# A cross-covariance attention and highway kernel: gates of two slots over two PSUM banks, v transposed as 32-bit words, a first chain that reads S from PSUM

## The chip, the cores and the metric

The kernel runs on one core of a Trainium2 chip, in one launch. The metric is the device time of that launch in microseconds. A median of several runs is given, and one further execution was recorded by the hardware profiler; all lines of the profile are of that one.

## The reference

```python
def _attn_ref(q, k, v, tau):              # q, k, v: (4, 6336, 256) float32
    qn = q / (norm(q, axis=1) + 1e-06)    # every channel is normed over the 6336 rows
    kn = k / (norm(k, axis=1) + 1e-06)
    s = kn.transpose(0, 2, 1) @ qn / tau  # (4, 256, 256): channel against channel
    a = softmax(s, axis=-1)
    return v @ a                          # (4, 6336, 256)

def _moe_ref(x, w_h, w_t, b_t):           # x: (25344, 256)
    H = np.maximum(x @ w_h, 0.0)
    T = 1.0 / (1.0 + np.exp(-(x @ w_t + b_t)))
    return T * H + (1.0 - T) * x
```

For each of four batches a 256x256 matrix of sums over all rows of q and k must be complete before the first row of that batch's output can be made. The output is then linear in v up to the gate: x = v a, h = v (a w_h), z = v (a w_t) + b_t, and out = sigmoid(z) relu(h) + (1 - sigmoid(z)) x.

## The kernel before

A batch has 6336 rows: 49 tiles of 128 rows and a rest of 64. Each partition holds 49 consecutive rows, so that a load of several tiles is one run of memory per partition. q, k and v are loaded as groups of tiles (QG, VG) through POOL's DMA queue, which turns f32 into f16 on the way; there are rings of four buffers for q, four for k and three for v. The output goes out through SP's queue, four slots (eight tiles) at a time.

The work on one batch has three parts.

- **Scores** (`emit_score`, L230, L234, L239): for each tile, S += k'q (two matmuls of 256 columns), and the diagonal blocks of the gram matrices of k and q in G (two matmuls of 128 columns each), whose diagonals are the squared norms. For some runs of four tiles (RUNS) the squares are made elsewhere: ACT squares (L448), POOL adds halves (L454), DVE reduces (L461), and PE adds the result up over the partitions at the end (L511). The last TAIL tiles of a batch do all q grams first, then all k grams, then all S.
- **The chain** (`make_chain`): norms from G (DVE, L502), their root (ACT in batch 0, POOL later), inverses (DVE), the inverse norms of q spread over the partitions by an f32 matmul (cq, L548), S copied to SBUF (ACT, L519), logits (DVE, L557), exponentials (ACT, L574), softmax rows into `mr` (DVE, L588), their transposes (PE, L599) and the products with w_h and w_t (PE, L618), copied to `mr` beside the softmax (L629). ACT changes its function table for the exponential and back (L490).
- **Slots**: a slot is a pair of tiles, 25 to a batch and 100 in all. For each, PE transposes v (`emit_transpose`, L293: four f16 matmuls against an identity into one PSUM bank, vtps), DVE or ACT copies that to SBUF (`emit_copy`, L307; ACT where the number of the slot is in ACT_COPY), PE makes z, h and x (`mains`, L317: four matmuls of 256 columns each), ACT makes the gate tt = sigmoid(z) (L358) and seeds the z bank with b_t again (L361), DVE makes o = relu(h) tt (L366) and ux = (tt - 1) x (L376), and POOL subtracts (L399) two slots at a time.

PSUM has eight banks of 2 KiB per partition: S, G, two z banks used in turn, one for vtps, and three (hx0, hx1, hx2) for h and x. S and G of batch 0 join those for h and x after the first chain; the scores of later batches take hx1 and hx2.

The order on each engine is written by a planner inside the kernel: it steps through time with a length for every task, keeps a list of tasks per kind and engine (`queues`), and at each step lets an engine take the first task of the first list that is ready (`step_pe`, `step_act`, `step_dve`, `step_pool`, `step_sp`). What it emits is then the fixed order of that engine. Chain tasks come first. PE then prefers scores up to the due slot (S_END), transposes some slots ahead (LOOKS), then z, h and x. POOL prefers loads to subtractions, and issues them in the list `order` (QOFF and VOFF set how early; the last lines before the sort set the first loads of batch 1, v and the weights). A load into a used buffer waits for the last reader of that buffer. Scores of batch 1 are interleaved with slots 0 to 21, and so on; from about slot 65 on there are slots alone.

Of the kernel before, what the change touches and what calls it, by code (L numbers as in the profile page):

```python
# [15 lines left out]
P = 128  # L16
# [44 lines left out]
def kernel(  # L61
# [33 lines left out]
    QG = [spans(4, 8, 8, 8, 8, 8, 3, 2), spans(4, 4, 12, 12, 12, 5)]  # L95
    QG += [spans(4, 8, 12, 12, 8, 5)] * (B - 2)
    VG = [spans(4, 8, 12, 12, 13)] + [spans(12, 12, 12, 13)] * (B - 1)
    GT = {"q": 12, "k": 12, "v": 13}
    CH = 4
    SQR = {"q": 4, "k": 2}  # L100
    RUNS = {1: {'q': [4, 8, 20, 32, 36, 44], 'k': [0, 8, 24, 28, 32, 40]}, 2: {'q': [0, 8, 12, 16, 20, 24, 28, 36, 40], 'k': [0, 12, 16, 32, 40]}, 3: {'q': [8, 12, 20, 28, 32, 40, 44], 'k': [0, 8, 16, 28, 32, 36]}}
    TAIL = [6, 12, 10, 7]
    SPARE = 0
    QOFF, VOFF = [1.5, 3.0, 4.0, 0.5], [7.5, 3.5, 0.5, 9.5]
    SAHEAD = [0, 0.5, 10.0, 10.5]
    LOOKS = [3, 3, 2, 2]
    HOLD = [2, 1, 1, 5]
    DVE_SUBS = 2
    SINGLES = 8
    ACT_COPY = {3, 14, 21, 22, 26, 34, 36, 39, 40, 44, 45, 51, 53, 54, 58, 61, 63, 64, 72, 77, 81, 83, 84, 88, 91, 96, 98, 99}  # L110
    NEAR = 2
    OUTST = 7
    QRING, VRING, ORING = 4, 3, 7
    TTR, UXR, VTR = 4, 3, 5
# [4 lines left out]
    S_END = [21.5, 42.5, 65.0]  # L119
# [35 lines left out]
    EXP_LAG = 0.6  # L155
# [57 lines left out]
    S_t, G_t = {}, {}  # L213
# [5 lines left out]
    def emit_score(b, j, parts, first, last):  # L219
        if first:  # L220
            tags = ("S", "G") if b == 0 else ("hx1", "hx2")
            S_t[b] = psum_pool.tile([P, 2, C], f32, tag=tags[0], name=f"S{b}")
            G_t[b] = psum_pool.tile([P, 4, P], f32, tag=tags[1], name=f"G{b}")
        nr = REM if j == NS else P
        kk, qq = tile_of("k", b, j), tile_of("q", b, j)
        S, G = S_t[b], G_t[b]
        for c in range(2):
            kc = kk[0:nr, bass.ts(c, P)]
# [4 lines left out]
            if "k" in parts:  # L233
                nc.tensor.matmul(  # L234
                    G[:, c, :], kc, kc, start=begins(b), stop=False, skip_group_check=True,
                )
        for c in range(2 if "q" in parts else 0):
            qc = qq[0:nr, bass.ts(c, P)]
            nc.tensor.matmul(  # L239
                G[:, 2 + c, :], qc, qc, start=begins(b), stop=False, skip_group_check=True  # L240
# [4 lines left out]
    def begins(b):  # L245
        if b in begun:
            return False
        begun.add(b)
# [4 lines left out]
    def make_scores(b):  # L253
# [3 lines left out]
        for parts in "qks":  # L257
# [26 lines left out]
    vT_ps, vT_t = {}, {}  # L284
    slot_of = {pair_of(t): t for t in range(NSLOT)}

    def emit_transpose(t):
        b, i = pair_of(t)
        ps = psum_pool.tile([P, 2, 2, P], f16, tag="vT", name=f"vtps{t}")
        for u, r in enumerate(nrows(i)):  # L290
            vt = tile_of("v", b, 2 * i + u)
            for c in range(2):
# [3 lines left out]
        vT_ps[t] = ps  # L296

    def emit_copy(t, e):
        i = pair_of(t)[1]
# [881 lines left out]
```

## Time and profile before

| what | value |
|---|---|
| median of 3 runs | 271.5 us (270.67 to 274.68) |
| the profiled execution | 270.55 us, of it span 268.8 us |
| PE busy | 246.3 us (92%), 2564 matmuls |
| DVE, ACT, POOL busy | 207.6, 192.9, 206.5 us |
| DMA | 66.08 MB as landed, share about 1 until some 228 us |
| granted TensorE clock | 0.996 |
| z, h and x matmuls (256 columns) | 1200, 273 ns each as recorded |
| transposes of v | 400, 219 ns each as recorded |

The span runs from the first to the last instruction that the profiler saw; the execution's own time is 1.75 us longer. A matmul's recorded length holds its latency, and matmuls overlap, so that the distance from one to the next is shorter than the record. In the lines that follow a group has its line of the kernel, engine, operation, output and inputs, shapes and count, then busy us and mean ns of one, then the idle time of its engine just before it with what ended it. A line of a table by stage has the stage's bounds, its length and for each engine busy us and count; then the granted clock, the share of the DMA engines and GB/s.

### The profile page before, as it was taken

To read this page: it belongs to the slowest core of one execution; us is meant where nothing else is said; L and a number is where in the kernel's file an instruction comes from. 1 tells how busy PE (TensorE), PEld (TensorE's weight loads), DVE (VectorE), ACT (ScalarE), POOL (GpSimd) and SP (SyncE) were. 2 spreads that over 40 slices of the span, in tenths; PEclk is the share of its full clock that TensorE was granted. 3 is DMA by queue.
4 is the path that set the end of the run, shared out by engine and by line. 5 is a ranking of instruction groups with operands and counts; after the bars stand their busy time and mean duration, and the time that the engine had idled before them with its cause. 6 is when DMAs were issued, how large, how long until landed. Compare 5 with 4: busy or idle time off the path is not lost.

```text
span 268.8 us, 6452 instructions
## 1 busy us (share of the span) xinstructions
PE 246.3 (92%) x2564; PEld 213.7 (79%) x2564; DVE 207.6 (77%) x414; ACT 192.9 (72%) x320; POOL 206.5 (77%) x183
## 2 busy tenths in 40 slices
PE   0996886999999999989999999999999999999990
PEld 0696784798889997879989987898988687999780
DVE  2000035869999999889989899889998998999894
ACT  3310025969689978879996798898868987888780
POOL 6133455399989999898899998899966485977880
PEclk9999999999999999999999999999999999999998
DMA  7999999999999999999999999999999999698435
GB/s 215 213 214 212 205 186 212 214 209 220 213 210 213 235 266 220 209 274 213 288 290 307 278 213 226 214 297 302 272 291 356 266 408 399 142 235 355 200 129 215
DMA packets 16143, 66.08 MB, mean 246 GB/s; under 512 B 1777, under 2 KB 4338, under 8 KB 13170
## 3 DMA queue, kind: packets, MB, share of 16 engines
q0 software_dynamic: 11040, 38.67, 73.0%
q1 hardware_dynamic: 4786, 26.22, 24.3%
q10 hardware_dynamic: 288, 0.79, 0.8%
q8 instruction: 20, 0.33, 0.4%
q14 instruction: 9, 0.07, 0.1%
HBM read 78.38 MB, written 25.95 MB: 388 GB/s over the span
## 4 chain that ended last, share of the span: by engine, by line
PE 47%; DMA 29%; POOL 9%; DVE 7%; ACT 3%; issue 3%; DVEq 0%; POOLq 0%; ACTq 0%
DMA k<-in_k_dram 24%; PE x L317 10%; PE h L317 9%; PE zbank L317 9%; PE S L230 7%; PE vtps L293 5%; POOL o L399 4%; DMA out_dram<-o 3%; PE G L234 3%; PE G L239 3%; DVE o L366 2%; DMA qk<-in_k_dram 2%; DVE ux L376 2%; ACT tt L358 1%; POOL q L177 1%
## 5 line engine op out<-in xcount | busy, mean ns | idle before, releaser
L399 POOL TENSOR_TENSOR o<-o,ux 128x1024 f32<-128x1024 f32 (+2 forms) x50 | 111.5, 2233 | 23.4 <-DVE ux L376 20.3
L317 PEld LDWEIGHTS <-vts 128*128 128x128 f16 x1200 | 111.7, 98 | 16.2 <-issue 4.1
L230 PE MATMUL S<-q,k 128*128 128x256 f16 x392 | 73.5, 278 | 12.5 <-ACT k L834 6.3
L358 ACT ACTIVATE tt<-zbank 128x512 f32<-128x512 f32 x100 | 59.4, 596 | 22.0 <-PE zbank L317 15.7
L366 DVE SCALAR_TENSOR_TENSOR o<-h,tt 128x512 f32<-128x512 f32 x96 | 65.6, 684 | 6.0 <-ACT tt L358 3.3
L376 DVE SCALAR_TENSOR_TENSOR ux<-tt,x 128x512 f32<-128x512 f32 (+1 forms) x104 | 68.0, 657 | 2.1 <-PE x L317 2.0
L317 PE MATMUL x<-mr,vts 128*128 128x256 f16 (+1 forms) x400 | 60.5, 273 | 0.3 <-DVE o L366 0.3
L317 PE MATMUL zbank<-mr,vts 128*128 128x256 f16 (+1 forms) x400 | 60.6, 273 | 0.0
L317 PE MATMUL h<-mr,vts 128*128 128x256 f16 (+1 forms) x400 | 60.5, 273 | 0.0
L361 ACT COPY zbank<-btb 128x512 f32<-128x512 f32 x98 | 57.6, 591 | 2.7
L230 PEld LDWEIGHTS <-k 128*128 128x128 f16 x392 | 37.5, 100 | 18.9 <-DMA k<-in_k_dram 7.8
L234 PE MATMUL G<-k 128*128 128x128 f16 x256 | 44.0, 224 | 0.7 <-DVE junk L502 0.7
L293 PE MATMUL vtps<-ident,v 128*128 128x128 f16 x392 | 38.3, 219 | 1.5 <-DVE vts L307 0.7
L307 DVE COPY vts<-vtps 128x512 f16<-128x512 f16 x68 | 28.6, 420 | 7.2 <-PE vtps L293 6.7
L293 PEld LDWEIGHTS <-v 128*128 128x128 f16 x392 | 28.7, 98 | 4.9 <-issue 1.7
L177 POOL DMA_DIRECT2D q<-in_q_dram x25 | 14.2, 570 | 23.0 <-PE G L239 18.6
L502 DVE SCALAR_TENSOR_TENSOR junk<-G,ident 128x128 f32<-128x128 f32 x16 | 4.7, 291 | 31.1 <-PE G L234 30.4
L239 PE MATMUL G<-q 128*128 128x128 f16 x216 | 28.6, 224 | 0.0
L454 POOL TENSOR_TENSOR sqq<-sqq 128x512 f32<-128x512 f32 (+1 forms) x22 | 26.5, 1207 | 0.1
L234 PEld LDWEIGHTS <-k 128*128 128x128 f16 x256 | 24.0, 101 | 1.8 <-issue 1.1
L448 ACT ACTIVATE sqq<-q 128x1024 f32<-128x1024 f16 x22 | 23.0, 1055 | 0.1
L461 DVE TENSOR_REDUCE sqq<-sqq 128x256 f32<-128x768 f32 x22 | 22.6, 1026 | 0.0
(78 smaller groups left out, 214.3 us busy)
## 6 DMA issues: line engine op xcount, KB each, us to landing
out_dram<-o SPq DMA_DIRECT2D x23, 1024.0 KB, 9.8
v<-in_v_dram POOLq DMA_DIRECT2D x11, 768.0 KB, 17.2
q<-in_q_dram POOLq DMA_DIRECT2D x7, 768.0 KB, 15.2
k<-in_k_dram POOLq DMA_DIRECT2D x7, 768.0 KB, 19.3
q<-in_q_dram POOLq DMA_DIRECT2D x9, 512.0 KB, 13.4
k<-in_k_dram POOLq DMA_DIRECT2D x9, 512.0 KB, 15.4
v<-in_v_dram POOLq DMA_DIRECT2D x4, 832.0 KB, 19.1
q<-in_q_dram POOLq DMA_DIRECT2D x4, 256.0 KB, 13.2
```

What stands on the lines that cost most here:

```text
L230: nc.tensor.matmul(S[:, c, :], kc, qq[0:nr, :], start=first and c == 0, stop=last and c == 1)
L234: nc.tensor.matmul(G[:, c, :], kc, kc, start=begins(b), stop=False, skip_group_check=True,)
L239: nc.tensor.matmul(G[:, 2 + c, :], qc, qc, start=begins(b), stop=False, skip_group_check=True)
L293: nc.tensor.transpose(ps[:, u, c, 0:r], vt[0:r, bass.ts(c, P)], ident[0:r, 0:r])
L307: cp(out=sb, in_=ps)
L317: nc.tensor.matmul(dst[0:r, u, :], vT_t[t][:, u, kt, 0:r], mr[:, kt, off : off + C], start=(not seeded and kt == 0 and (u == 0 or i == NPA ...
L358: nc.scalar.activation(out=tts[t], in_=zbank[t % 2], func=Act.Sigmoid)
L361: nc.scalar.copy(out=zbank[t % 2], in_=btb)
L366: nc.vector.scalar_tensor_tensor(out=ot[pr, o0 + us.start : o0 + us.stop, :], in0=hx["h", t][pr, us, :], scalar=0.0, in1=tts[t][pr, us, :] ...
L376: nc.vector.scalar_tensor_tensor(out=uxs[n][pr, 2 * half + us.start : 2 * half + us.stop, :], in0=tts[t][pr, us, :], scalar=1.0, in1=hx["x ...
L399: ins = sub.tensor_tensor(out=dst, in0=dst, in1=uxs[n][pr, us, :], op=AluOp.subtract)
L454: nc.gpsimd.tensor_tensor(out=sq[:, 1 : 1 + half, :], in0=sq[:, 1 : 1 + half, :], in1=sq[:, 1 + CH - half : 1 + CH, :], op=AluOp.add,)
```

## The change

- **Words.** In batches 0 to 2 v is transposed as f32 words, each of which holds two neighbouring f16 channels: two matmuls of 128 columns per slot instead of four. The channels of k are read with a step of two in these batches, so that the rows of `mr` match (`channels`). The transposes of two slots share one bank and are copied by one instruction, in batch 3 too (f16 there).
- **Batch 3 by DMA.** 22 tiles (11 slots) of batch 3's v are transposed from SBUF to SBUF by six DMAs on SP's queue (DT, `emit_dt`), into buffers of the q and k rings.
- **Gates and seeds.** z has one tile over two banks. A gate, and a seed, covers two slots in one instruction of 128x1024, except for the pairs in ZSPLIT (27 of 50 for the gate).
- **Chain.** The copy of S is gone; the logits read S in PSUM, and cq is copied instead (cqs, on the engine in SPREAD). The q grams of batch 0 have a bank of their own (hx0). The engines of the other copies are set by CENG.
- **Squares.** Other runs (32 instead of 39), and the number of tiles that POOL adds is set per batch (POOLED): 17 additions instead of 39.
- **Lists and numbers.** Groups of loads are cut anew (85 loads of q, k and v by POOL instead of 67), the first loads have another order (FIRSTS), PE's list of z is kept apart from that of h and x, and most of the planner's numbers are new.

```diff
-    QG = [spans(4, 8, 8, 8, 8, 8, 3, 2), spans(4, 4, 12, 12, 12, 5)]
-    QG += [spans(4, 8, 12, 12, 8, 5)] * (B - 2)
-    VG = [spans(4, 8, 12, 12, 13)] + [spans(12, 12, 12, 13)] * (B - 1)
+    QSZ = [[4, 6, 1, 9, 3, 1, 11, 1, 4, 9], [5, 4, 6, 5, 10, 3, 5, 11], [5, 7, 10, 10, 4, 6, 7], [12, 5, 2, 11, 6, 7, 6]]
+    VSZ = [[4, 1, 7, 8, 5, 11, 13], [12, 12, 12, 13], [12, 9, 4, 3, 8, 3, 10], [11, 13, 7, 5, 13]]
+    QG = [spans(*x) for x in QSZ]
+    VG = [spans(*x) for x in VSZ]
+    REM_AT = 4.5
+    FIRSTS = ['q11', 'q10', 'v00', 'w', 'remv']
     GT = {"q": 12, "k": 12, "v": 13}
+    DT = [(0, 4), (12, 6), (20, 2), (24, 4), (40, 4), (44, 2)]
+    DT_FROM = 67
+    WORDS = [True] * (B - 1) + [not DT]
...
+    POOLED = {1: [0, 1], 2: [2, 1], 3: [0, 0]}
...
+    SPREAD = ['ACT', 'DVE', 'DVE', 'ACT']
+    MARGIN = 1.2
+    CENG = ['AAAD', 'DADA', 'DADD', 'AADD']
+    TAIL = [13, 8, 10, 8]
...
-    TTR, UXR, VTR = 4, 3, 5
+    TTR, UXR, VTU = 2, 3, 3
+    ZSPLIT = {1, 4, 7, 8, 12, 13, 16, 21, 22, 23, 24, 25, 26, 29, 33, 34, 35, 37, 38, 41, 42, 43, 44, 45, 46, 47, 49}
...
+    words = lambda b: WORDS[b]
+
+    def channels(ap, kind, b, c):
+        if kind == "k" and words(b):
+            return ap.rearrange("p (i two) -> p two i", two=2)[:, c, :]
+        return ap[:, bass.ts(c, P)]
...
+            Gq_t[b] = G_t[b][:, 2:4, :] if b else psum_pool.tile(
+                [P, 2, P], f32, tag="hx0", name=f"Gq{b}"
+            )
...
-            kc = kk[0:nr, bass.ts(c, P)]
+            kc = channels(kk[0:nr, :], "k", b, c)
...
+    def emit_dt(n):
+        s0, ns = DT[n]
+        kind = "qk"[n % 2]
+        g = group_of(VG[B - 1], s0)
+        o = s0 - VG[B - 1][g][0]
+        assert o + ns <= VG[B - 1][g][1]
+        vt = stream_pool.tile([P, GT[kind], C], f16, tag=f"{kind}_in", bufs=QRING, name=f"vtd{n}")
+        ins = nc.sync.dma_start_transpose(
+            out=vt[:, 0:ns, :].rearrange("p s (c r) -> p (s c) r", c=2),
+            in_=tiles["v", B - 1, g][:, o : o + ns, :].rearrange("p s c -> p (s c)"),
+        )
+        for m in range(ns):
+            vT_dma[s0 + m] = vt[:, m, :].rearrange("p (c r) -> p c r", c=2)
+        return ins
...
+            if words(b):
+                vT_ps[n] = psum_pool.tile([P, 4, P], f32, tag="vT", name=f"vtps{n}")
+            else:
+                vT_ps[n] = psum_pool.tile([P, 4, 2, P], f16, tag="vT", name=f"vtps{n}")
+        ps = vT_ps[n][:, 2 * half : 2 * half + 2]
         for u, r in enumerate(nrows(i)):
             vt = tile_of("v", b, 2 * i + u)
-            for c in range(2):
+            if words(b):
+                nc.tensor.transpose(
+                    ps[:, u, 0:r], vt[0:r, :].bitcast(f32), ident0[0:r, 0:r]
+                )
+            for c in range(0 if words(b) else 2):
                 nc.tensor.transpose(
...
+            m = 2 * len(copies[n])
+            cp(out=sb[:, 0:m], in_=ps[:, 0:m])
+        vT_t[n] = sb.bitcast(f16).rearrange("p u (r c) -> p u c r", c=2) if words(b) else sb
...
-    def emit_tt(t):
-        tts[t] = work_pool.tile([P, 2, C], f32, tag="tt", bufs=TTR, name=f"tt{t}")
-        nc.scalar.activation(out=tts[t], in_=zbank[t % 2], func=Act.Sigmoid)
-
-    def emit_seed(t):
-        nc.scalar.copy(out=zbank[t % 2], in_=btb)
+    def emit_tt(slots):
+        if slots[0] % 2 == 0:
+            tt = work_pool.tile([P, 4, C], f32, tag="tt", bufs=TTR, name=f"tt{slots[0]}")
+            for m in range(2):
+                tts[slots[0] + m] = tt[:, 2 * m : 2 * m + 2, :]
+            whole[slots[0]] = tt
+        if len(slots) == 2:
+            nc.scalar.activation(out=whole[slots[0]], in_=zbank[0], func=Act.Sigmoid)
+        else:
+            t = slots[0]
+            nc.scalar.activation(out=tts[t], in_=z_of(t), func=Act.Sigmoid)
+
+    def z_of(t):
+        return zbank[0][:, 2 * (t % 2) : 2 * (t % 2) + 2, :]
+
+    def emit_seed(slots):
+        if len(slots) == 2:
+            nc.scalar.copy(out=zbank[0], in_=btb.to_broadcast([P, 4, C]))
+        else:
+            nc.scalar.copy(out=z_of(slots[0]), in_=btb.to_broadcast([P, 2, C]))
...
-        def ssb(e):
-            st["ssb"] = work_pool.tile([P, 2, C], f32, tag="ssb", bufs=1, name=f"ssb{b}")
-            nc.scalar.copy(out=st["ssb"], in_=S_t.pop(b))
+        def spread(e):
+            st["cqs"] = work_pool.tile([P, C], f32, tag="cqs", bufs=1, name=f"cqs{b}")
+            cp = nc.vector.tensor_copy if e == "DVE" else nc.scalar.copy
+            cp(out=st["cqs"], in_=st["cq"][:, 0, :])
...
-                    out=st["ssb"][:, c, :], in0=st["ssb"][:, c, :], in1=st["cq"][:, 0, :],
+                    out=st["ssb"][:, c, :], in0=S_t[b][:, c, :], in1=st["cqs"],
...
-            if kind == "q":
-                add("ssb", "ACT", 0.62, ssb, [(last_score[b], PE_LAG)])
...
+        add("cq", "PE", 4 * MM(C), pe_cq, [(T["invs", "q"], TO_PE)], bank=lambda: [T["cqs"]])
+        add("cqs", SPREAD[b], 0.35, spread, [(T["cq"], PE_LAG)])
+        if SPREAD[b] == "ACT":
+            queues["ACT.chain"][-2:] = queues["ACT.chain"][:-3:-1]
         for c in range(2):
-            add(("logits", c), "DVE", 0.38, logits(c), [(T["cq"], PE_LAG), (T["ssb"], LAG)])
+            add(("logits", c), "DVE", 0.38, logits(c),
+                [(T["cqs"], LAG), (last_score[b], PE_LAG)])
...
-    order += [(-94.5, "remq", 0, 0), (-94.5, "remk", 0, 0)]
-    order += [(-80, "q", 1, 0), (-80, "k", 1, 0), (-65, "q", 1, 1), (-65, "k", 1, 1)]
-    order += [(-78, "w", 0, 0), (-78, "w", 0, 1)]
-    order += [(-70, "v", 0, 0), (-69, "remv", 0, 0), (2, "remq", 0, 1), (2, "remk", 0, 1)]
+    at = len(QG[0]) - 100 - REM_AT
+    order += [(at, "remq", 0, 0), (at, "remk", 0, 0), (2, "remq", 0, 1), (2, "remk", 0, 1)]
+    for n, what in enumerate(FIRSTS):
...
+    for n in range(NSLOT // 2):
+        both = [2 * n, 2 * n + 1]
+        for kind, made, emit, split in (
+            ("tt", TT, emit_tt, n in ZSPLIT),
+            ("seed", SEED, emit_seed, n in ZSPLIT or n - 1 in ZSPLIT),
+        ):
+            for slots in ([[t] for t in both] if split else [both]):
+                task = Task((kind, slots[0], len(slots)), "ACT", 0.61 if split else 1.05,
+                            lambda e, slots=slots, emit=emit: emit(slots))
+                for t in slots:
+                    made[t] = task
+                if kind == "tt" or n > 0:
+                    queues["ACT." + kind].append(task)
...
-        queues["PE.out"] += [Z[t], H[t], X[t]] if t < NSLOT - 1 else [H[t], X[t]]
-        if t == NSLOT - 1:
-            queues["PE.out"].insert(len(queues["PE.out"]) - 3, Z[t])
-        queues["PE.T"].append(TR[t])
-        queues["copy"].append(CP[t])
-        queues["ACT.tt"].append(TT[t])
+        queues["PE.z"].append(Z[t])
+        queues["PE.out"] += [H[t], X[t]]
...
-        if take("PE.out", "PE", now):
+        if take("PE.z", "PE", now) or take("PE.out", "PE", now):
```

## Prediction

> **What bounds the kernel now.** I read the page's busy times first, then a table by stage (cut where every tenth slot's x ends), then the chain that ended last, the groups by shape, and last the timeline of the first chain.
>
> ```profile
> PE 246.3 (92%) x2564; PEld 213.7 (79%) x2564; DVE 207.6 (77%) x414; ACT 192.9 (72%) x320; POOL 206.5 (77%) x183
> ```
>
> PE is busiest, but a busy PE says little, since overlapping matmuls are counted with their latency. The pitch is what counts. The chain gives it:
>
> ```profile
> 56.24 0.44 PE x L317 x4
> ...
> 84.20 0.45 PE G L234 x8
> ```
>
> So a matmul of 256 columns takes its turn in 0.110 us (0.44/4) and one of 128 columns in 0.056 us (0.45/8). With these I price everything that PE does from the first zbank matmul (46.2 us) to the last x (261.7 us), counted in the program's own order: 1484 of 256 columns (z, h, x and S) 163.2 us, 272 grams and 388 transposes 37.0, three chains about 7.3: together 207.5 us. The stages of that stretch last 215.5 us:
>
> ```profile
> core 0: us, PE busy (x) PEld busy (x) DVE busy (x) ACT busy (x) POOL busy (x), PEclk, DMA share, GB/s
> 46.21:68.05 21.84, 21.29 (x232) 18.98 (x230) 17.66 (x31) 18.53 (x30) 17.34 (x16) 1.00 1.06 214
> 68.05:90.62 22.57, 22.54 (x249) 20.24 (x246) 21.85 (x36) 18.54 (x28) 21.58 (x16) 1.00 1.06 214
> 90.62:119.91 29.29, 27.82 (x281) 23.62 (x279) 25.92 (x58) 24.38 (x40) 28.07 (x30) 1.00 1.03 242
> ...
> 230.50:244.80 14.30, 14.30 (x151) 13.02 (x150) 13.45 (x25) 12.82 (x24) 12.20 (x8) 1.00 0.92 229
> 244.80:261.70 16.90, 16.90 (x168) 14.04 (x166) 15.45 (x32) 13.86 (x25) 14.20 (x11) 1.00 0.50 197
> sum 215.49, PE 212.07 PEld 185.18 DVE 197.53 ACT 181.58 POOL 187.66; mean PE 21.21 PEld 18.52 DVE 19.75 ACT 18.16 POOL 18.77
> ```
>
> The reader is to see three things. PE loses only 8.0 us here (215.5 - 207.5), most of it where batch 1's chain runs (90.6 to 119.9). DVE and POOL stand at 88 to 97% in most rows, so they can hold PE up. DMA is full (a share over 1) until the last rows. PE's total work is therefore the first price, its 8 us of waits the second, and the 46.2 us ahead of the first slot the third; behind the last x lie 7.1 us.
>
> **The change, part by part.**
>
> *Transposes on PE.* Behind the first zbank matmul 332 of the 388 f16 transposes go (44 of them to the DMA): 332 x 0.056 = -18.6 us. 146 transposes of f32 words come. The trace has none; the nearest rows are f32 matmuls of the same 128x128 shape (L548), beside the f16 transposes (L293):
>
> ```profile
> L293 PE MATMUL vtps<-ident,v 128*128 128x128 f16 x392 | 38.3, 219 | 1.5 <-DVE vts L307 0.7 <-DMA v<-in_v_dram 0.5 <-DVE ux L376 0.2
> L293 PEld LDWEIGHTS <-v 128*128 128x128 f16 x392 | 28.7, 98 | 4.9 <-issue 1.7 <-DMA v<-in_v_dram 1.5
> ...
> L548 PE MATMUL cq<-ident_tau,inv 128*128 128x128 f32 x16 | 2.6, 283 | 0.4 <-DVE inv L542 0.4
> L548 PEld LDWEIGHTS cq<-ident_tau,inv 128*128 128x128 f32 x16 | 2.1, 190 | 0.6 <-PE x L317 0.6
> ```
>
> Sixteen records for eight f32 matmuls: each runs as two passes, with weight loads of 190 ns against 98. Four passes took 0.61 us at 99.33, one alone 0.275, so the pitch of a pass is (0.61 - 0.275)/3 = 0.112 us. Bounds for one word transpose: 0.056 (as cheap as an f16 one) and 0.224 (both passes). I take one pass, 0.112, because a transpose only moves bits: 146 x 0.112 = +16.4. The Trainium skill, "TensorE: Matmul & The Clock Gate", section "Terms", says that transpose mode is four times faster for FP32; by that the price falls to the lower bound and the sum by 8.2 us. The same page, section "Weight-path perf modes", says FP32 weights get no fast load, which the 190 against 98 ns bears out and which speaks for a price above it.
>
> *Fewer squares off PE.* 39 runs become 32, so 52 more grams behind the first slot: 52 x 0.056 = +2.9; two S matmuls fewer there, -0.2. PE in all: -18.6 + 16.4 + 2.9 - 0.2 = **+0.5 us**. Half of each word is a channel, so k and the copied v are now read with a step of two. No row has a stepped PE operand. Bounds: nothing, or what f32 adds to a moving pass (275 - 222 = 0.053 us) on the 120 k-grams of batches 1 and 2, +6.4 us. I take nothing: the operand stays f16, and the f16 row is the nearest.
>
> *Other engines, which cost only where PE waits for them.* DVE's copies: 68 x 0.420 and small ones (2.0) against 27 f32 pairs at 0.688 (the 128x512 f32 cast, L629), 6 f16 pairs at about 0.75 and 0.9 of small ones: 30.6 to 24.0 us. ACT: 18 copies of 0.58 fewer (-10), 7 squares of 1.055 fewer (-7.4), four copies of S (-2.3) against two of cq; 36 gates or seeds in pairs at about 1.05 against 1.19 (-5). POOL: its adds fall from 46.6 us to 16 (17 instead of 39, ten of them small), and 18 more loads of 0.56 us are issued (+10.1): -20 us net, though in POOL's queue each load now stands ahead of subtractions more often. Reductions that lose their POOL half get longer on DVE, 3 tiles at 1.03 us against 5 at about 1.55; over the 32 runs that is +2. So ACT and POOL are eased by some 20 us each, DVE by 3 to 5. What does that buy? At most PE's 8.0 us of waits. I take half, **-3.9 us**, bounds 0 and -8.0: waits of a chain on itself stay.
>
> A gate for two slots takes both banks: 1.05 + 1.05 us pass before PE may write z again, against 16 x 0.110 + 0.45 = 2.2 us of h, x and transposes of the two slots. That covers it barely; with the steps between engines it could cost about 0.5 us at the four joint gates that come after the last scores (slots 72, 78, 80, 96), up to +2. Scores cover the others. I take 0.
>
> *DMA transposes.* Six, 1.4 MB, on SP's queue, between stores. The nearest rows are stores: 2.6 us for 256 KB at the end, 5.4 for 128 KB in the full queue. At 215 GB/s the bytes take 6.7 us of DMA time; the last two rows above leave 9.6 us of it free. Stores queued behind a transpose wait with it, and next for them the output buffers (seven). 0 if they land ahead of their slots; +3 if the last two, which need batch 3's last load, are late. I take 0. The Trainium skill, "VectorE: DVE Perf Modes", section "The three transpose paths", gives 1309 ns for a 128x128 block by DMA; 44 blocks one after another would be an estimated 58 us, far beyond that cover; no row here can show it.
>
> *The first chain.* Its rows (PE, ACT):
>
> ```profile
> 38.52 0.59 ACT L519 COPY ssb<-S 128x512 f32<-128x512 f32 x1 [1.77 <-PE S L230]
> 39.23 1.28 ACT L490 ACT_TABLE_LOAD   x1
> 40.63 0.46 ACT L574 ACTIVATE cq<-ssb,inv 128x256 f32<-128x256 f32 x1
> 43.02 0.28 PE L230 MATMUL S<-q,k 128*128 128x256 f16 x1 [0.75 <-DMA k<-in_k_dram]
> 45.98 0.40 PE L293 MATMUL vtps<-ident,v 128*128 128x128 f16 x4 [0.48 <-DMA v<-in_v_dram]
> ```
>
> The last S ends at 38.7; the copy holds k's root, that the table load, and that the exponentials to 40.63. Without the copy and with the q sums in a bank of their own, roots and table load fall under the S matmuls of the tail; exponentials start at 38.7 + 0.2 + 0.41 (one logits product) = 39.4: -1.2. The tail of 13 tiles costs 26 x 0.056 + 26 x 0.110 = 4.4 us behind the last k against 3.9 now: +0.5. The two waits for DMA in the chain (0.75 ahead of "at", 0.48 ahead of the first z) are avoided by a wider margin and smaller first v groups: -1.2. Against that, 18 tiles of q and k now go ahead of v and the weights, where 8 did: ten more tiles of 64 KB at 213 GB/s are 3 us, less the 4 that moved behind; most of it passes under the chain. Sum **-2.0**, bounds -2.4 and +0.7.
>
> **Sum.** 268.8 + 0.5 - 3.9 - 2.0 = 263.4 us of span. The profiled execution took 270.55, 1.75 more than its span: **265.1**, 2.0% under its own 270.55 and 2.4% under the median of 271.5.
>
> **Rivals.** *Words for the price of f16 transposes* (0.056): 8.2 us less, 257. But DMA was full to 215 us, and the last two rows leave it only 9.6 us, of which the transposes want 6.7; so about 260. For it: a transpose does no arithmetic. Against: the 190 ns loads.
>
> *The waits come back.* The eased engines were not what PE waited for; DMA was (shares over 1), and joint gates or late DMA transposes add 2 to 3 us. Then no 3.9, half of the 2.0, and +2: 268.8 + 0.5 - 1.0 + 2 + 1.75 = 272; without the +2, 270. For it: transfer bytes are the same and come in more pieces.
>
> *Slower: a word transpose runs both passes*, as every f32 matmul in the trace does. 146 x 0.112 more on the engine that bounds: 265.1 + 16.4 = 281.5. It beats the gain from (270.55 - 265.1)/146 = 0.037 more, 0.149 us each. Against: passes split a number in order to multiply it.
>
> **How the numbers follow.** Forecast 0.50 (own range 262 to 268.5), cheap words 0.17, waits back 0.19, two passes 0.14. About 2% is what a measurement can tell from no change here: 266.1 and 276.9 around 271.5. Some 0.31 of the forecast's 0.50 lies below 266.1; with the cheap words faster has 0.48; two passes give slower 0.14; the rest, 0.38, is within. The range reaches from 258.5 (cheap words) to 273.5 (waits back, with the late transposes), and leaves out the two passes and a little below.
>
> **What would show it.** One weight load and one matmul record per word transpose, at a pitch near 0.11; the first zbank matmul near 44 us; PE's waits from there to the last x near 4 us; no PE wait for DMA transposes behind slot 75. Two records per word, a first z after 46 us, or waits above 8 us would make it wrong.

## The result and the profile after

The changed kernel takes 302.5 us (median of 4 runs, 301.3 to 303.6) against 272.8 us (270.7 to 274.7) for the kernel before in the same session: a ratio of 1.109 with a 95% interval of 1.099 to 1.120. The forecast was 265.1 us with a range of 258.5 to 273.5, so it was wrong in sign and in size. The profiled execution took 303.6 us, of it span 301.8. Some executions of a kernel run at a lower granted clock and take over 1.5% longer than its fastest one; the medians and ratios below leave those out.

The page of the changed kernel, busy times:

```profile
PE 256.2 (85%) x2426; PEld 217.3 (72%) x2426; DVE 226.1 (75%) x370; ACT 172.3 (57%) x260; POOL 187.3 (62%) x179
```

ACT and POOL have lost 20 us each, as forecast. DVE has gained 18.5 us where 3 to 5 less were forecast. The table by stage, cut again where every tenth slot's x ends:

```profile
core 0: us, PE busy (x) PEld busy (x) DVE busy (x) ACT busy (x) POOL busy (x), PEclk, DMA share, GB/s
51.00:75.60 24.60, 23.24 (x228) 20.68 (x229) 19.54 (x25) 18.68 (x25) 18.54 (x21) 1.00 1.10 211
75.60:102.00 26.40, 23.58 (x233) 20.40 (x230) 26.40 (x29) 16.74 (x23) 18.11 (x16) 1.00 1.05 219
...
130.90:155.50 24.60, 23.31 (x230) 20.72 (x227) 24.37 (x33) 15.69 (x20) 21.20 (x19) 1.00 0.97 220
...
185.90:213.60 27.70, 25.23 (x259) 22.29 (x259) 27.15 (x31) 13.63 (x19) 16.79 (x14) 1.00 0.91 236
...
255.40:276.50 21.10, 16.32 (x150) 13.51 (x149) 15.86 (x25) 12.70 (x21) 13.41 (x8) 1.00 0.90 274
276.50:294.50 18.00, 15.45 (x132) 11.67 (x130) 13.85 (x25) 10.71 (x19) 12.84 (x10) 1.00 0.34 135
sum 243.50, PE 219.84 PEld 186.66 DVE 216.78 ACT 160.99 POOL 168.30; mean PE 21.98 PEld 18.67 DVE 21.68 ACT 16.10 POOL 16.83
```

The rows of the kernel before for slots 30 to 40, 50 to 60 and 70 to 80, for comparison:

```profile
120.07:141.12 21.05, 21.05 (x233) 19.11 (x232) 19.84 (x32) 19.34 (x31) 19.47 (x14) 1.00 1.05 264
...
169.82:190.62 20.80, 20.54 (x219) 18.62 (x219) 19.64 (x33) 18.98 (x30) 19.47 (x14) 1.00 1.03 282
...
215.21:231.14 15.93, 15.93 (x159) 13.34 (x158) 14.74 (x31) 12.70 (x23) 12.26 (x8) 1.00 0.89 361
```

The 33.0 us of span divide into three places. The first z comes at 51.0 instead of 46.2 us (+4.8). The stages of slots 10 to 20, 30 to 40 and 50 to 60 last 26.4, 24.6 and 27.7 us where they lasted 22.6, 21.0 and 20.8 (+14.3 together), and in these DVE is busy to 98 to 100%. Slots 70 to 100, where no scores are left, last 58.2 instead of 47.3 us (+10.9), with no engine full: PE is busy 77 to 86%. What is left (+3.0) is spread over the other stages and the tail.

The waits of PE, with the total, the number and the longest, tell what stops it in the last place:

```profile
PE S L254 <- DMA k<-in_k_dram: 8.0, 2, 5.9
PE zbank L402 <- ACT tt L451: 6.8, 14, 0.9
PE zbank L402 <- ACT zbank L460: 6.7, 17, 0.7
...
PE vtps L368 <- DVE vts L392: 4.2, 6, 1.1
```

Neither of the two zbank lines stood in the list of before. The chain that ended last shows them as a closed ring (start, length, what):

```profile
263.28 0.61 PE zbank L402 x4
...
263.97 0.60 ACT zbank L460
...
264.59 0.60 ACT tt L451
...
265.23 0.61 PE zbank L402 x4
```

One turn, from 263.28 to 265.23, is 1.95 us and serves one slot. Before, the chain in slots without scores was PE's own work alone, 1.53 us a slot. The order is the point: the seed of one half (L460) starts when PE has written z of the *other* half, and PE's next z when the gate of the other half is done. Two halves of two different banks behave like one. ACT's seeds say the same (kernel before, then changed kernel; the last numbers are the idle time just before them and what ended it):

```profile
L361 ACT COPY zbank<-btb 128x512 f32<-128x512 f32 x98 | 57.6, 591 | 2.7
...
L460 ACT COPY zbank<-btb 128x512 f32<-128x512 f32 x74 | 43.6, 590 | 12.9 <-PE zbank L402 11.1
```

What fills DVE in the full stages is above all one group, its reductions:

```profile
L562 DVE TENSOR_REDUCE sqk<-sqk 128x256 f32<-128x1024 f32 x9 | 17.8, 1975 | 0.0
L562 DVE TENSOR_REDUCE sqq<-sqq 128x256 f32<-128x1280 f32 x7 | 16.9, 2408 | 0.0
L562 DVE TENSOR_REDUCE sqk<-sqk 128x256 f32<-128x1280 f32 x5 | 12.0, 2397 | 0.1
L562 DVE TENSOR_REDUCE sqq<-sqq 128x256 f32<-128x768 f32 x7 | 7.2, 1026 | 0.0
...
L562 DVE TENSOR_REDUCE sqq<-sqq 128x256 f32<-128x1024 f32 x2 | 3.9, 1951 | 0.0
L562 DVE TENSOR_REDUCE sqk<-sqk 128x256 f32<-128x768 f32 x2 | 2.0, 1022 | 0.0
```

Three tiles (768 elements) still take 1.03 us, but four take 1.95 to 1.98 and five 2.40. The sum is 59.7 us for 32 runs, against 40.1 for 39 runs before.

And the words, which were the forecast's largest term:

```profile
L368 PE MATMUL vtps<-ident,v 128*128 128x128 f32 x147 | 27.6, 277 | 4.2 <-DVE vts L392 4.2
```

There is one record each, and in the timeline four of them take 0.60 us: (0.60 - 0.277)/3 = 0.108 us apart, against the 0.112 assumed.

### The profile page after: what moved, and what is told of

Same layout as the page of the kernel before. It is cut to its first block, busy times and chain, and to the rows that moved or that the text cites. A ratio compares the mean times of both kernels' runs of the same rounds, so it can differ in the third digit from the quotient of the medians.

```text
span 301.8 us, 6078 instructions
## 1 busy us (share of the span) xinstructions
PE 256.2 (85%) x2426; PEld 217.3 (72%) x2426; DVE 226.1 (75%) x370; ACT 172.3 (57%) x260; POOL 187.3 (62%) x179
## 4 chain that ended last, share of the span: by engine, by line
PE 41%; DVE 23%; ACT 19%; DMA 7%; issue 7%; POOL 1%; DVEq 0%; ACTq 0%
PE zbank L402 12%; PE S L254 8%; ACT zbank L460 7%; ACT tt L451 6%; DMA k<-in_k_dram 6%; DVE sqk L562 5%; PE x L402 5%; DVE o L465 5%; PE h L402 4%; DVE ux L475 4%; DVE sqq L562 4%; PE G L258 2%; PE vtps L368 2%; ACT tt L448 2%; DVE vts L392 2%
## 5 line engine op out<-in xcount | busy, mean ns | idle before, releaser
L402 PEld LDWEIGHTS <-vts 128*128 128x128 f16 (+1 forms) x1068 | 102.4, 98 | 31.6 <-issue 19.4
L402 PE MATMUL zbank<-mr,vts 128*128 128x256 f16 (+1 forms) x356 | 49.0, 273 | 9.7 <-ACT zbank L460 5.3
L460 ACT COPY zbank<-btb 128x512 f32<-128x512 f32 x74 | 43.6, 590 | 12.9 <-PE zbank L402 11.1
L451 ACT ACTIVATE tt<-zbank 128x512 f32<-128x512 f32 x54 | 30.9, 594 | 27.0 <-PE zbank L402 21.9
L448 ACT ACTIVATE tt<-zbank 128x1024 f32<-128x1024 f32 x23 | 23.5, 1024 | 36.3 <-PE zbank L402 28.1
L562 DVE TENSOR_REDUCE sqk<-sqk 128x256 f32<-128x1024 f32 (+2 forms) x16 | 31.8, 1987 | 0.1
L368 PE MATMUL vtps<-ident,v 128*128 128x128 f32 x147 | 27.6, 277 | 4.2 <-DVE vts L392 4.2
L562 DVE TENSOR_REDUCE sqq<-sqq 128x256 f32<-128x1280 f32 (+2 forms) x16 | 27.9, 1746 | 0.0
L392 DVE COPY vts<-vtps 128x512 f32<-128x512 f32 (+2 forms) x33 | 22.4, 678 | 5.0 <-PE vtps L368 2.8
L263 PEld LDWEIGHTS <-q 128*128 128x128 f16 x264 | 22.2, 102 | 2.5
L263 PE MATMUL G<-q 128*128 128x128 f16 x166 | 22.4, 222 | 0.0
```

The lines of the kernel that those rows point to most:

```text
L263: nc.tensor.matmul(Gq[:, c, :], qc, qc, start=begins(b, "q"), stop=False, skip_group_check=True)
L368: nc.tensor.transpose(ps[:, u, 0:r], vt[0:r, :].bitcast(f32), ident0[0:r, 0:r])
L402: nc.tensor.matmul(dst[0:r, u, :], vT_of(t, u)[:, kt, 0:r], mr[:, kt, off : off + C], start=(not seeded and kt == 0 and (u == 0 or i == NP ...
L448: nc.scalar.activation(out=whole[slots[0]], in_=zbank[0], func=Act.Sigmoid)
L451: nc.scalar.activation(out=tts[t], in_=z_of(t), func=Act.Sigmoid)
L460: nc.scalar.copy(out=z_of(slots[0]), in_=btb.to_broadcast([P, 2, C]))
```

## The experiments

Three theories followed. *Ring*: z as one tile makes each half wait for the other. *Reductions*: DVE's longer sums fill the stages with squares. *First loads*: the changed lists delay the first z. Medians in us; ratios are to the kernel before in the same session. Stages are cut at every tenth slot's x.

**Ring.** First all gates and seeds single, then z as two tiles besides.

```diff
-    ZSPLIT = {1, 4, 7, 8, ...}
+    ZSPLIT = set(range(50))
```

> The changed kernel with every gate and seed of one slot alone (ZSPLIT holds all 50 pairs), z still one tile over two banks. Theory 1 (the two halves of the one z tile wait for each other: z, seed of the other half, gate, next z in a ring of 1.95 us) expects no gain, 299 to 308 us: the ring stays, and more slots are in it. Rival (a gate for two slots at once holds up PE, because both banks are taken for 2.05 us) expects 288 to 296. Theory 2 (DVE's reductions of four and five tiles) and theory 3 (the first loads) expect 300 to 304.

Measured: 307.0, 1.135 [1.130, 1.140]. Single gates do not help: with z as one tile they add 4.5 us.

```diff
-        return zbank[0][:, 2 * (t % 2) : 2 * (t % 2) + 2, :]
+        return zbank[t % 2][:, :, :]
...
-        zb = psum_pool.tile([P, 4, C], f32, tag="z", name="zbank")
+            zb = psum_pool.tile([P, 2, C], f32, tag=f"z{m}", name=f"zbank{m}")
```

> As a_all_single, but z is two tiles of one bank each. Theory 1 expects slots 70 to 100 to fall from some 56 us to 46 to 48, and 2 to 6 us more to come out of the stages before: 285 to 292 us, 10 to 17 us under a_all_single. Theories 2 and 3 expect no difference from a_all_single beyond 2 us.

Measured: 287.2, 1.061 [1.055, 1.068]. That is 19.8 us less from the tile alone, and slots 70 to 100 fall from 58.5 to 46.2 us. The converse, in the kernel before:

```diff
-            zb = psum_pool.tile([P, 2, C], f32, tag=f"z{i}", name=f"zbank{i}")
+        z_both = psum_pool.tile([P, 4, C], f32, tag="z", name="zbank")
...
+            zb = z_both[:, 2 * i : 2 * i + 2, :]
```

> The kernel before with one edit: z is one tile over two banks instead of two tiles. No instruction is added, and gates and seeds stay single. Theory (ring): a seed now waits for PE's z of the other slot and z for the other slot's gate, so that a slot takes at least 1.95 us where nothing else takes that long: 35 slots without scores from about 1.5 to about 1.9 to 2.0 us each, +14 us, and +2 to +6 in the slots with scores, 285 us, range 280 to 292, with idle time of PE in front of zbank ended by ACT of 15 us or more. Rival (the ring shows only in the order of the changed kernel, where gates, seeds and z are queued in pairs): 271 to 275.

Measured: 288.0, 1.063 [1.058, 1.068], so +17.4 us with the same instructions in the same order on every engine. Slots 70 to 100 take 60.0 us. PE's waits there name the ring:

```profile
PE zbank L317 <- ACT zbank L361: 11.5, 32, 0.9
```

**Reductions.** POOL's half is given back in the changed kernel, and taken away in the kernel before.

```diff
-    POOLED = {1: [0, 1], 2: [2, 1], 3: [0, 0]}
+    POOLED = {1: [2, 2], 2: [2, 2], 3: [2, 2]}
```

> The changed kernel, but POOL adds two tiles ahead of every reduction, as it did before (POOLED all 2), so that DVE reduces three tiles at 1.03 us instead of four at 1.96 or five at 2.41. Theory 2 expects DVE's reductions to fall from 59.7 us to some 33, and the stages of slots 10 to 20, 30 to 40 and 50 to 60, in which DVE is busy throughout, to get 8 to 14 us shorter: 288 to 295 us. Theory 1 expects slots 70 to 100 unchanged at 56 us, and on its own 300 to 304.

Measured: 292.0, 1.078 [1.074, 1.081], 10.5 us less. Slots 10 to 20, 30 to 40 and 50 to 60 take 22.7, 22.4 and 26.1 us, so that the reductions account for 7.5 of the 14.3 us found there. Slots 50 to 60 come down to 22.4 us only with the lists of before (below).

```diff
-        half = 1 if first else 2
+        half = 0
...
-        queues["POOL.add"].append(ad)
```

> The kernel before with one edit: POOL adds no halves, and DVE reduces all tiles of a run (4 in the first run of a batch, 5 in the others, 39 runs in all). Theory (a reduction of 4 and 5 tiles takes 1.96 and 2.40 us as in the changed kernel, and DVE is the bound in the stages with scores): 6 x 1.96 + 33 x 2.40 = 91 us of reductions instead of 40, DVE +51 us, of which DVE had some 10 us free in those stages: +35 to +45, 306 to 316 us, with POOL at 160 us. Rival (the long reductions of the changed kernel were slow because POOL and DVE used one memory port at the same time; with POOL's additions gone they take 1.55 us as forecast): reductions 60 us, the time 280 to 292.

Measured: 321.4, 1.186 [1.180, 1.193]; +50.7 us, more than the highest expected. The reductions take 89.9 us in all, at 1.95 and 2.37 us each, with no addition on POOL at all: it isn't POOL's additions beside them that make them long. The planner was told the new length (2.2 us), so the order on the engines changed as well, and the +50.7 us are not the reductions' length alone. PE waited for DVE's copies of v and for each batch's sums:

```profile
PE vtps L293 <- DVE vts L307: 13.2, 9, 2.4
PE G L510 <- DVE sqq L461: 12.0, 3, 6.4
```

In these stages its clock falls too (table by stage; the clock is the third number from the right):

```profile
91.80:141.30 49.50, 36.67 (x325) 29.96 (x323) 45.38 (x64) 32.46 (x50) 20.67 (x25) 0.86 1.04 261
...
241.90:280.40 38.50, 23.91 (x186) 17.86 (x184) 29.80 (x58) 17.80 (x33) 14.53 (x11) 0.73 0.51 141
```

Then the operation by itself, without any other work on the chip.

> Not the kernel's work: DVE alone adds up 2, 3, 4, 5, 6 and 8 tiles of 128x256 in f32, six times each, the tiles 1024 or 1056 bytes apart, and 4 neighbouring elements in a row; all else is left out. Theory (the jump from 1.03 us at 3 tiles to 1.95 at 4 comes from the number of terms of each sum): the same durations at both distances, 2 tiles below 0.8 us, 6 tiles near 2.8, 8 near 3.7, and 4 neighbours as long as 4 tiles. Rival (the distance of 1024 bytes between the terms is at fault, above 3 of them): the tiles 1056 bytes apart take 1.34 ns an element throughout, 1.37 us at 4 and 1.72 at 5. Other rival (POOL's and PE's work beside it is at fault): 4 tiles at 1.37 us here in every arrangement.

Groups of this run, tiles 1024 bytes apart (a) or 1056 (wide); L58 adds four neighbouring elements:

```profile
L54 DVE TENSOR_REDUCE o<-a 128x256 f32<-128x2048 f32 x6 | 21.9, 3644 | 0.0
...
L52 DVE TENSOR_REDUCE o<-a 128x256 f32<-128x1280 f32 x6 | 13.8, 2305 | 0.0
L51 DVE TENSOR_REDUCE o<-a 128x256 f32<-128x1024 f32 x6 | 11.3, 1878 | 0.0
L56 DVE TENSOR_REDUCE o<-wide 128x256 f32<-128x1024 f32 x6 | 11.3, 1878 | 0.0
L58 DVE TENSOR_REDUCE o<-a 128x256 f32<-128x1024 f32 x6 | 7.3, 1213 | 0.0
...
L50 DVE TENSOR_REDUCE o<-a 128x256 f32<-128x768 f32 x6 | 6.2, 1026 | 0.0
L49 DVE TENSOR_REDUCE o<-a 128x256 f32<-128x512 f32 x6 | 4.1, 675 | 0.0
```

Two, three, four, five and eight tiles cost 0.68, 1.03, 1.88, 2.31 and 3.64 us. The step is between three and four at both distances (five tiles 1056 bytes apart took 2.41 us), and four neighbours take only 1.21 us. So no expectation was wholly right: it is the number of terms together with their lying apart. The Trainium skill, "Vector Engine (DVE) Microarchitecture Reference", section "5.2 Measured stream behaviour on trn2 (trn3 not measured)", gives 1.73 ns an element where one source hops with every element (by 4 KiB there), 1.054 where it does not, and about 75 ns an instruction. An estimate from it, 1024 x 1.73 + 75 = 1.85 us for four tiles, 3.62 for eight and 1.15 for four neighbours, is close to the rows above; for two and three tiles it gives 0.96 and 1.40 us, and there the rows decide.

**First loads.** Batch 0's groups, tail and rest of before, with the order of the first loads still that of the change.

```diff
-    QSZ = [[4, 6, 1, 9, 3, 1, 11, 1, 4, 9], ...
+    QSZ = [[4, 8, 8, 8, 8, 8, 3, 2], ...
-    REM_AT = 4.5
+    REM_AT = 2.5
-    TAIL = [13, 8, 10, 8]
+    TAIL = [6, 8, 10, 8]
```

> The changed kernel with batch 0's groups of loads and its tail as before (4, 8, 8, 8, 8, 8, 3, 2; tail of 6 tiles). Theory 3 (the first z came at 51.0 us instead of 46.2 because a group of 11 tiles landed at 28.4 us in one lump, behind which PE had 25 tiles to score) expects the first z at 45 to 47.5 us and the whole at 296.5 to 299.5. Theories 1 and 2 expect no more than that anywhere else.

Measured: 301.7, 1.113 [1.111, 1.116]; first z at 49.0 us, 2.0 us earlier, and 0.8 us less in all. Mostly a miss, to be taken up again below.

**Both repairs, then the lists, then the DMA transposes.** Two z tiles and POOL's halves together:

> The changed kernel with both repairs at once: z in two tiles of one bank each (all gates and seeds single) and POOL's half of the additions back. Theory (the ring over z and the longer reductions are two causes in different stages, the one mostly in slots 0 to 10 and behind slot 60, the other in slots 10 to 60): the gains add up, 302.5 - 14 - 10 = 278 us, range 275 to 282, with the stages of slots 10 to 40 some 6 us shorter than with two z tiles alone and the slots behind 70 unchanged at about 14.7 us for ten. Rival (both only hid a third limit, DMA or the loads in smaller groups): the second repair brings under 4 us on top of the first, 284 or more.

Measured: 280.4, 1.033 [1.027, 1.039]: most of the two gains adds up (the second brings some 7 us on top of the first, 10.5 alone). Then all lists of before (groups, RUNS, TAIL, FIRSTS, REM_AT, QOFF, VOFF, SAHEAD, S_END):

> As the run with both repairs, and besides the groups of loads, the runs of squares, the tail lengths, the order of the first loads and the due times of the loads and scores are those of the kernel before. What is left of the change: words, pair copies, DMA transposes, no copy of S, one tt tile for two slots. Theory (the first loads of the change, 18 tiles ahead of v and the weights, cost the 4.8 us at the first z, and the rest of the forecast stands): first z back near 45 to 46 us, and the whole 264 to 271 us. Rival (words, the shared tt tile or DMA transposes cost on their own): first z near 46 but the whole above 274, with the stages of slots 70 to 100 or those with scores longer than before.

Measured: of four executions one took 275.1 us at a mean clock of 0.994; three took 279.3 to 281.6 us at 0.965 to 0.972, the profiled one 280.75. First z at 47.2. So the theory missed its number; the rival's time came (above 274), its first z near 46 did not. In the profiled execution the chain that ended last names what is late:

```profile
232.30 10.04 DMA v<-in_v_dram
...
242.36 8.77 DMA vtd<-v
...
251.18 1.89 PE zbank L402 x8
```

With the groups of before, the last load of v lands at 242.4 us and its transposes 8.8 us after, when slots want them. PE was busy only 0.88 of 2 us meanwhile, and then its clock stood at 0.50 to 256 us: eight z matmuls took 1.89 us where they take 0.88 otherwise. Without DMA transposes (DT empty, words in batch 3 too):

> As the run with the lists of before, and besides no DMA transposes: batch 3's v is transposed by PE as words like the others. 22 more words cost PE 22 x 0.112 = 2.5 us. Theory (in the run with the lists of before the last v load lands at 242.4 us and its transposes 8.8 us later, which holds PE, and the clock falls afterwards): the stage of slots 80 to 90 falls from 20.9 to about 15.5, the whole is 271 to 275 us. Rival (DMA transposes cost nothing but that one wait, and PE's extra work and the copies eat the gain): 277 or more.

Measured: 275.1, 1.015 [1.011, 1.020]. Slots 80 to 90 take 15.3 us, against 21.8 in the profiled execution before it. But the quick execution of that run took 275.1 us too. So the late transposes and the low clock behind them are what the long execution shows, and that DMA transposes cost time as such is not shown.

**What was left.** In place of words, f16 transposes; and a tt tile for each slot.

> As the run without DMA transposes, but every transpose of v is of f16 (four of 128 columns to a slot, two slots to a bank and a copy), and k and v are read without a step. PE's transposes cost 392 x 0.056 = 22.0 us against 198 x 0.112 = 22.2 us. Theory (words cost PE as much as what they replace, and stepped operands are free): within 3 us of the run without DMA transposes. Rival (the stepped operands or the longer weight load of a word, 141 against 98 ns, cost PE time that the records hide): faster by 4 us or more. Other rival (the shorter copies of words matter): slower by 4 us or more.

Measured: 274.8, 1.014 [1.011, 1.018], equal to its counterpart to 0.3 us: a word costs PE what the two f16 transposes cost that it replaces.

> As the run without DMA transposes, but with a tile of tt for each slot, as before, in place of one for two slots. Theory (two slots in one tile of SBUF couple the two gates only loosely, since two such tiles hold four slots): within 2 us. Rival (the shared tile makes a gate wait for ux of the slot beside it as z did in PSUM): faster by 4 us or more.

Measured: 273.4, 1.010 [1.006, 1.013], 1.6 us less. The theory's bound of 2 us holds. This is the fastest version with words that was run; it is still slower than the kernel before.

Its first z came at 47.0 us. The timeline showed the table load behind cqs in ACT's queue, and the copies of at (the transposed softmax rows) behind the second table load. So these went to DVE:

```diff
-    SPREAD = ['ACT', ...
-    CENG = ['AAAD', ...
+    SPREAD = ['DVE', ...
+    CENG = ['DDAD', ...
```

> As the run with single tt tiles, with the first chain's copies moved: cqs on DVE, so that nothing stands between the root and the table load in ACT's queue, and the two copies of at on DVE, so that they need not wait for ACT's second table load. Theory (the forecast's gain of the first chain was lost in ACT's queue, where the table load stood behind the copy of cq and the copies of at behind the return of the table, and then to the clock, which fell to 0.50 behind the idle stretch): the products with the weights go ahead of the scores that wait for k at 43.3 us, first z at 45 us or earlier instead of 46.96, clock 1.00 in 40 to 50 us, and 1.5 to 2.5 us less in all, 271 to 272 us. Rival (the first chain waits for the weights or v): first z at 46.5 or later and the time within 1 us of 273.4.

Measured: 274.6, 1.011 [1.008, 1.014]. The mechanism is as expected and the time is not. In the timeline the exponentials begin at 39.2 and z at 44.18 us:

```profile
37.46 1.28 ACT L587 ACT_TABLE_LOAD   x1
...
39.20 0.48 ACT L672 ACTIVATE e<-ssb,inv 128x256 f32<-128x256 f32 x1 [0.24 <-DVE ssb L657]
...
44.18 1.03 PE L402 MATMUL zbank<-mr,vts 128*128 128x256 f16 x8
```

But slot 10 ends at 69.3 us, against 69.1 in the run before it and 68.2 in the kernel before. The 2.8 us turned into a wait, in the stretch of 44 to 70 us:

```profile
PE S L254 <- DMA k<-in_k_dram: 2.2, 1, 2.2
```

The k load that ends it lands at 53.2 us; the one on the chain of the kernel before landed at 53.4. The DMA engines are full in this stretch (share 1.06), so an earlier slot 0 only waits longer for the same load.

> As the run with the first chain's copies moved, with f16 transposes in place of words. Theory (words and f16 cost PE the same): within 1.5 us of it, either way. Rival (word transposes keep PE's clock low behind idle stretches): the clock is 1.00 throughout here while the run with words dips, and this one is 1.5 us or more faster.

Measured: 278.1, 1.023 [1.018, 1.028]: slower by 3.5 us, against both expectations. Three of the six executions took 276.1 to 276.5 us at a clock of 0.991 to 0.994, the other three 279.8 us at 0.971 to 0.976. Even the quick ones are 1.7 us slower than the median with words, whose clock was 0.981 to 0.997, so the rival fails: words are not what lowers the clock. Why this order of instructions lost more was not followed up.

> As the run with the first chain's copies moved, with the planner's look-ahead numbers of the kernel before (how many slots are transposed ahead, how long z is held, how many loads are open). Theory (engines with room to spare leave nothing for these numbers to gain; PE's own work of 207.5 us sets the time): within 2 us of it. Rival (the new numbers hold PE up): 268 us or less.

Measured: 287.0, 1.060 [1.056, 1.064]. Both theories miss: with few slots transposed ahead, pairs come too late, and PE waits for the copies:

```profile
PE zbank L402 <- DVE vts L392: 10.2, 11, 1.5
```

The next three expectations start from a table that had missed some of the x matmuls. Counted in full, slot 70 of the last run ended at 218.4 us and not at 212.2, level with 218.7 in the run with the chain's copies moved: there was no early gain to keep.

> As the run with the planner's numbers of before, but with the changed kernel's numbers for batch 3 (slots transposed ahead 4 in place of 2, hold 3 in place of 5). In the run with all of before's numbers slot 70 ended at 212.2 us, 5.4 us ahead of the run with the first chain's copies moved, and then slots without scores took 2.0 us each with PE waiting 10.2 us for DVE's copies. Theory (the numbers of before suit the stages with scores, those of the change the slots at the end, where a pair is transposed and copied two slots ahead): slots 70 to 100 back to about 48 us, the whole 266 to 270 us, the first version below the kernel before and near the forecast of 265.1. Rival (the early gain is a debt of stores, loads or subtractions that the end pays anyway): 273 or more.

> As the run before it with one number more from the change: DVE's copies are taken up to 4 slots ahead in place of 2. If the wait for DVE's copies comes from how late they are taken rather than how late they are transposed, this one has the gain of slots 70 to 100 and the other has not: 266 to 270 us against 275 or more. If the stages with scores lose by early copies on DVE, slot 70 ends at 217 us again and the whole takes 273 or more.

> As the run with batch 3's numbers of the change, but with its look-ahead of 4 slots for batch 2's slots too (50 to 74), since there the stage of slots 70 to 80 still took 22.4 us, with PE waiting 3.2 us for DVE's copies; and two more copies at the end on ACT (copies 41 and 47). Theory (the wait is for transposes that come too late for a pair): slot 70 stays near 212 us, slots 70 to 80 fall to about 16, the whole 267 to 271 us, at or a little below the kernel before. Rival (DVE, busy for over 93% of the end, is the bound there and the gain ahead of it is paid back): slots 70 to 100 take 50 us or more, or slot 70 ends at 217, and the whole takes 273 or more.

Measured: 277.8, 279.9 and 274.7 (ratios 1.026, 1.031 and 1.014). Look-ahead takes away the wait, and the rest stays where it was: as the rival of the last one has it, slots 70 to 100 take 50.9 us there. That DVE is the bound there, as that rival says, is not shown: it is busy for 45.5 of these 50.9 us. None of these beats the kernel before.

## Why the prediction was wrong, step by step

Of its own signs of being wrong two came: a first z after 46 us (51.0), and waits above 8 us (PE's named waits from the first z to the last x add up to 23.3 us). The way from 302.5 us to the forecast's 265.1, in the order of the runs: 22.1 us by the two repairs, with gates and seeds single (280.4), 5.3 by the lists of before (275.1, one execution), 1.7 by single tt tiles (273.4), and 8.3 that no run took away.

**"Joint gates cost 0, up to +2."** This step failed by the most. It priced how long a gate holds two banks, and never asked what one *tile* over two banks does to the slots with single gates. The tile alone costs 17.4 us in the kernel before and 19.8 in the changed one; joint gates in place of single ones, with z as one tile, saved 4.5. The diff says that gates and seeds of either half now name the same tile. That waits go by the tile no row of before could show; it was a rival to be named, and the two runs with one z tile against two show it.

**"3 tiles at 1.03 us against 5 at about 1.55; over the 32 runs that is +2."** The measured term is +19.6 us on DVE (59.7 against 40.1). The prediction does not say where its 1.55 came from; the trace had reductions of one size only, 3 tiles. Giving POOL's halves back saves 10.5 us alone and some 7 beside the other repair, since the term falls on the engine that the table by stage showed at 88 to 97%. The forecast looked at DVE's total and not at those stages.

**"At most PE's 8.0 us of waits; I take half, -3.9."** The 8.0 us are what the rows lasted beyond PE's work at its pitch. The waits that the profile of before names in that stretch add up to 3.8 us, and none of them is for ACT or POOL. The two longest:

```profile
PE S L230 <- DMA k<-in_k_dram: 2.0, 3, 1.0
PE vtps L293 <- DMA v<-in_v_dram: 0.5, 1, 0.5
```

So little could be bought from ACT and POOL. They were eased by 20 us each, as worked out, and it bought nothing. In the version with all three causes gone (one z tile, longer reductions, changed lists; the run with single tt tiles), PE takes 218.4 us from first z to last x, 2.1 more than before (216.3). What PE waited for there were loads and DVE, not ACT or POOL.

**"First chain -2.0."** Measured +4.8. Two things were missed. In ACT's queue cqs stood ahead of the table load; moved away, z came at 44.18 us, where the forecast had put it (46.2 - 2.0). And with the changed lists PE waits 4.7 to 5.9 us for the group of eleven k tiles that lands near 28 us, in the changed kernel and in the four runs with these lists (single gates, two z tiles, POOL's halves, both). The clock falls there to 0.50 to 0.67, and first z lay between 47.0 and 51.0 us. What makes that spread stays open: batch 0's groups of before brought 2.0 us (49.0), but with both repairs first z came at 47.0 with the changed lists and at 47.2 with those of before. That -2.0 was worth nothing in the end, as the k load of batch 1 shows; a term for what meets the work next was missing.

**DMA transposes at 0.** Right for the changed kernel: no PE wait names them. With the groups of before the last ones landed late in the profiled execution (8.8 us after issue), but the quick execution of that run equals the run without them, so no cost is shown.

**PE's own work, +0.5.** Right. One record per word, 0.108 us, and words against f16 equal to 0.3 us. With it fall the two rivals on the price of a word, 0.056 and two passes. The Trainium skill, "TensorE: Matmul & The Clock Gate", section "Terms", calls transpose mode four times faster for FP32; here a word at 0.108 us is about twice as fast as the two passes of an f32 matmul (0.224).

Added up for the version with all three causes gone: the prediction's rows end at 261.70 us, but the last x ends at 262.54. With that, the forecast had z at 44.2, 212.9 us to the last x, and 8.0 behind it. It measured 47.0, 218.4 and 8.1, that is 2.8 + 5.4 + 0.1 = 8.3 us over 265.1. Of these, 2.0 and 3.9 are the two gains that did not come; the places of the other 2.4 us the runs don't settle.

The rival "waits come back" has nearly the time of that last version (272, measured 273.4), by luck: its +2 was for joint gates or late DMA transposes, which that version does not have. And for the changed kernel no rival had the ring or the reductions. The slower cases that were weighed lay in PE's price of a word and in waits for DMA; both causes lay in what other engines must wait for or do longer.

## What to carry to other kernels

Before two buffers are made one, list who reads and writes each half, and ask of every instruction whether it now waits for the other half: in this program a tile is what is waited for, not a bank. When an operation grows past the sizes in the trace, don't draw a line through one point; measure it, or bound it by the steepest neighbour. And a stage in which DMA is full can take back what is gained ahead of it, as it did here.

## What the runs showed of the hardware

- A DVE sum over tiles that lie apart costs some 0.35 us a tile up to three (0.675, 1.026) and then jumps by 0.85 us at the fourth (1.878). Folding five tiles to three with an addition of 128x512 on DVE itself took 0.682 us in the same run, so 0.68 + 1.03 = 1.71 us would be an estimate for five tiles instead of 2.31; that was not tried in the kernel.
- PE's granted clock falls to 0.50 without a full stop. In the run with single tt tiles PE was busy 0.91 of 2 us and 1.00 of 2 us, and its clock came to 0.50; in the run with f16 in place of words it was busy as little and kept 1.00 (tables by stretch of the one and the other, columns as above):

```profile
40.00:42.00 2.00, 0.91 (x6) 0.53 (x6) 1.25 (x5) 1.98 (x6) 1.46 (x3) 1.00 1.15 216
42.00:44.00 2.00, 1.00 (x7) 0.70 (x8) 0.54 (x1) 1.17 (x4) 1.06 (x2) 0.73 1.10 222
44.00:46.00 2.00, 2.00 (x9) 0.83 (x7) 0.14 (x1) 0.59 (x1) 0.08 (x1) 0.50 1.06 217
```

```profile
40.00:42.00 2.00, 0.91 (x10) 0.56 (x10) 1.04 (x4) 1.97 (x7) 1.66 (x3) 1.00 1.15 205
42.00:44.00 2.00, 1.04 (x8) 0.63 (x9) 0.76 (x2) 1.39 (x4) 1.11 (x2) 1.00 1.09 219
44.00:46.00 2.00, 2.00 (x22) 1.64 (x21) 0.69 (x1) 0.59 (x1) 0.03 (x1) 1.00 1.08 221
```

What decides between the two stays open. The Trainium skill, "TensorE: Matmul & The Clock Gate", section "What's actually happening", speaks of half rate after an idle window of some 3.4 us; in the run with single tt tiles PE was never idle for more than 1.0 us at a stretch between 36 and 48 us.
